# Gated mix of two linear attentions: output weights of two tiles at once on row halves, rows of r by block, small products of G as filler

## The chip, the core and the metric

The kernel runs on one core of one Trainium2 chip. The metric is the device time of one execution in microseconds; the figure before is the median of three runs.

## What is computed

Two linear-attention branches A and B read the same x (2048 rows, 640 features, bfloat16), each with weights of its own; a gate of each row mixes their outputs.

```python
H = 32; Dh = D // H                      # D = 640, so 20 features a head
q, k, v = split(x @ wqkv)                # each [S, H, Dh]
phi = lambda t: where(t > 0, t + 1, exp(t)) + 1e-6
pq, pk = phi(q), phi(k)
kv = einsum("bhsd,bhse->bhde", pk, v)
z = einsum("bhsd->bhd", pk)
num = einsum("bhqd,bhde->bhqe", pq, kv)
den = einsum("bhqd,bhd->bhq", pq, z)[..., None] + 1e-6
branch = (num / den).reshape(B, S, D) @ wo
...
g = sigmoid((x * gate_w).sum(-1, keepdims=True))
return g * branch_A + (1 - g) * branch_B
```

## The kernel before, in words

The value projection is never computed for all rows. Since v = x Wv, the kernel forms G = xT pk (640 x 640, tile GT) from x and the feature map of the keys (PK), then M = GT Wv (m_part), masks M to the heads (tile MG, by a constant in CB), and multiplies by the output weights wo. The result, WP, is a 640 x 640 matrix a branch, and the output is the feature map of the queries (PQ), scaled by gate / denominator, times WP. That factor of a row and a head is called r.

Stages, in the order in which TensorE runs them:

- Keys (k_part, k_tile): for each of 16 row tiles of 128 rows and each branch, x times Wk; ScalarE takes the exponential (EK), VectorE finishes PK.
- Queries (q_tile, L505): for each branch, four blocks of 512 rows and five feature tiles k, one tile of PQ. Feature tiles 0 to 3 take every second column of Wq (tile_of, L399), so that the tiles of a pair share one layout of heads over the partitions. WQ is loaded in one transfer a branch.
- G of A (g_piece, L543) is mixed in between the query tiles. A row-block j of G has four pieces q; one piece is four row tiles, each a 512- and a 128-column matmul. After the last piece ScalarE copies the block into GT.
- Sum z of the keys: GpSimd adds the 16 tiles of PK (z_add, L565), and z_turn (L575) spreads the sum over partitions with five small matmuls.
- The chains of L922 place what follows around the pieces of G of B: after its first piece z_turn of B and M of A (m_part, L718); after its second wp_a_den (L905): output weights of A (wp_tile, L747) with the denominators of both branches (den, L639) between them, then reciprocals, tables and widening, which use no TensorE. The remaining 18 pieces of G of B follow.
- wp_tile forms one of five feature tiles of WP: for each of two column halves of 320, four matmuls of 80 rows and 32 output columns on four column strips of the array, each for one window w of heads. ScalarE copies the first half out of PSUM, VectorE the second.
- r: VectorE takes the reciprocals (recip), SP writes them to a table in DRAM with five copies of each row (table), and reads them back repeated over the partitions (widen, L687): three issues for the first block of 512 rows, three for the other three blocks together, for each branch. scale (L699) multiplies PQ by it, block by block, in two VectorE instructions.
- Output (fin_mm, L792): row tiles 0 to 3 do A and B apart: A's part is copied to TA by ScalarE (fin_a) and added when B's is copied out (fin_out); later tiles sum ten products in one group. fin_pp picks the PSUM pair. A, t = 0 and 1, come first, then M of B, A t = 2, the output weights of B, A t = 3, then B t = 0 to 3 and tiles 4 to 15.

The order on each engine is the order in the program, and the scheduler (_Sched) puts in the waits from the keys that each operation reads and writes. All reads of PSUM by ScalarE and VectorE count as writes of the bank. L292 is the matmul of every stage (helper mms), L281 the DMA issue of every load (helper dma), so groups on the page go by tiles. PSUM has eight banks; pair i is banks 2i and 2i + 1.

Of the kernel before, what the change touches and what calls it, by code (L numbers as in the profile page):

```python
# [11 lines left out]
S = 2048  # L12
# [17 lines left out]
W = 80  # L30
HS = (0, 3, 6, 9, 12, 16, 19, 22, 25, 28)
PAD = DH * HS[-1] + 128 - D

# [12 lines left out]
def _build_consts():  # L46
    cd = np.zeros((128, C_W), dtype=np.float32)
    p = np.arange(128)[:, None]
    f = np.arange(64)[None, :]
    for w in range(NW):  # L50
        assert HS[w] <= 64 * w // DH and (64 * w + 63) // DH < HS[w] + W // DH <= H
        cd[0:W, C_MK + 64 * w : C_MK + 64 * w + 64] = (HS[w] + p // DH == (64 * w + f) // DH)[0:W]
    for k in range(NC):
        head = (512 + p if k == 4 else 256 * (k // 2) + 2 * p) // DH
        cd[:, C_ZM + 32 * k : C_ZM + 32 * k + 32] = head == np.arange(32)[None, :]
    return _bf16_bits(cd)
# [136 lines left out]
def bass_gated_mix__linear_attn_block__linear_attn_block__prompt_kernel(  # L193
# [20 lines left out]
    with ExitStack() as es:  # L214
        E = es.enter_context

        def sb(name, shape, dtype=dt.bfloat16):
# [11 lines left out]

        WVF = {X: sb("WV" + X, [128, NC * D + PAD]) for X in BR}  # L230
        WV = {X: WVF[X][:, 0 : NC * D].rearrange("p (c f) -> p c f", c=NC) for X in BR}
# [6 lines left out]
            "A": PK["A"][:, 0:10, :].rearrange("p t f -> p (t f)")[:, 0 : 3 * S].rearrange("p (i n) -> p i n", i=3),  # L238
            "B": XT[:, 0:3, :],
        }  # L240
        RX_LAP = {
            "A": [("PK", "A", t) for t in range(10)],
            "B": [("XT", t, c) for t in range(NT) for c in range(3)],
# [3 lines left out]
        MG = sb("MG", [W, NW, 64])  # L247
# [77 lines left out]
        def wo_at(X, w):  # L325

            if X == "A":
                Y = BR[w // NC]
                return WK[Y][0:W, w % NC, 0:D], ("WK", Y, w % NC)
            if w < NC:  # L330
                return WQ["A"][0:W, w, :], ("WQ", "A")
            return PK["A"][0:W, 6 + w, :], ("PK", "A", 6 + w)

        def load_wo(eng, X, w):
            o, key = wo_at(X, w)
            r0 = DH * HS[w]
            dma(eng, "wo%s%d" % (X, w), o, wo[X][r0 : r0 + W, :], writes=[("WO", X, w), key])
# [24 lines left out]
        for X in BR:  # L362
            pool(lambda e, X=X: e.memset(WVF[X][:, NC * D : NC * D + PAD], 0.0), writes=[("WVP", X)])
# [27 lines left out]
        load_w("SP", "wqA", WQ["A"], wqkv["A"][:, 0:D], ("WQ", "A"))  # L391
# [4 lines left out]
        load_w("SP", "wqB", WQ["B"], wqkv["B"][:, 0:D], ("WQ", "B"))  # L396
        load_w("SP", "wvB", WV["B"], wqkv["B"][:, 2 * D : 3 * D], ("WV", "B"))

        def tile_of(row, k):  # L399

            return row[:, 512:D] if k == 4 else row[:, 256 * (k // 2) + k % 2 : 256 * (k // 2) + 256 : 2]
# [103 lines left out]
        def q_tile(X, b, k):  # L505
# [7 lines left out]
                reads=xt_reads(4 * b, 4 * b + 4) + [("WQ", X)],  # L513
# [29 lines left out]
        def g_piece(X, j, q, pp):  # L543
            P = PP[pp]
            bks = [("PS", 2 * pp), ("PS", 2 * pp + 1)]
            steps = []
            for t in range(4 * q, 4 * q + 4):
                l = XN[:, t, 128 * j : 128 * j + 128]
                steps.append((P[:, 0:512], l, PK[X][:, t, 0:512], t == 0, t == NT - 1, None))
                steps.append((P[:, 512:D], l, PK[X][:, t, 512:D], t == 0, t == NT - 1, None))  # L550
            mms(
                steps,
                reads=[("XN", t) for t in range(4 * q, 4 * q + 4)] + [("PK", X, t) for t in range(4 * q, 4 * q + 4)],
                writes=bks,
                name="g%s%d%d" % (X, j, q),
            )
            if q == 3:
                act(
                    lambda e: e.activation(GT[:, j, :], P[:, 0:D], ACT.Copy),
                    reads=bks,  # L560
                    writes=[("GT", j)],
                )


        def z_add(X, t, pace=()):  # L565
            xi = BR.index(X)
            a = PK[X][:, 0, :] if t == 1 else ZS[:, :]
            o = ZP[:, xi, :] if t == NT - 1 else ZS[:, :]
            pool(
                lambda e: e.tensor_tensor(out=o, in0=a, in1=PK[X][:, t, :], op=ALU.add),  # L570
# [416 lines left out]
```

## Time and profile before

| | us |
|---|---|
| runs (three) | 191.35, 191.59, 192.03 |
| median | 191.59 |
| the profiled execution | 190.99 |
| its span | 189.7 |

The page counts time from the span's start. Idle time of an engine that is not on the chain of waits costs nothing. The busy rows of the other engines around the change, by form (busy us, mean ns, then idle time and its releaser):

```profile
L518 ACT ACTIVATE EQ<-ps 128x512 bf16<-128x512 f32 x40 | 23.9, 597 | 34.1 <-PE ps L292 34.0
L831 DVE CAST OSTG<-ps 128x640 bf16<-128x640 f32 x11 | 9.1, 826 | 14.8 <-PE ps L292 14.8
L559 ACT ACTIVATE GT<-ps 128x640 bf16<-128x640 f32 x10 | 7.0, 704 | 19.8 <-PE ps L292 19.8
L704 DVE TENSOR_TENSOR PQA<-PQA,PKA 128x2048 bf16<-128x2048 bf16 x4 | 4.9, 1217 | 5.9 <-DMA PKA<-rsA 5.9
L669 DVE RECIPROCAL RCA<-DTA 128x128 bf16<-128x128 f32 x4 | 3.4, 906 | 0.0
L767 DVE CAST WPB<-ps 128x320 bf16<-128x320 f32 x5 | 2.1, 482 | 1.2 <-PE ps L292 1.2
L767 ACT ACTIVATE WPB<-ps 128x320 bf16<-128x320 f32 x5 | 1.8, 447 | 2.3 <-PE ps L292 2.3
L737 DVE TENSOR_TENSOR MG<-ps,CB 80x512 bf16<-80x512 f32 x2 | 1.4, 687 | 6.4 <-PE ps L292 6.4
L737 DVE TENSOR_TENSOR MG<-ps,CB 80x128 bf16<-80x128 f32 x2 | 0.6, 277 | 0.0
```

And the transfers: KB each, median us from issue to landing.

```profile
PKA<-rsA SPq DMA_DIRECT2D x3, 384.0 KB, 4.0
XT<-rsB SPq DMA_DIRECT2D x3, 384.0 KB, 6.0
WKB<-in_B_wqkv_dram SPq DMA_DIRECT2D x1, 800.0 KB, 6.7
WQA<-in_A_wqkv_dram SPq DMA_DIRECT2D x1, 800.0 KB, 6.1
...
rsA<-RCA SPq DMA_DIRECT2D x4, 160.0 KB, 2.7
...
PKA<-rsA SPq DMA_DIRECT2D x3, 128.0 KB, 2.8
XT<-rsB SPq DMA_DIRECT2D x3, 128.0 KB, 3.4
...
gd<-SG SPq DMA_DIRECT2D x2, 8.0 KB, 15.6
...
WKB<-in_gate_w_dram SPq DMA_DIRECT2D x1, 1.2 KB, 6.7
```

### The profile page before, as it was taken

Reading aid. Unit: us, or ns where it says so; the run is one execution under the profiler, and the core shown is the slowest. Engines: PE = TensorE matmul, PEld = TensorE weight load, DVE = VectorE, ACT = ScalarE, POOL = GpSimd, SP = SyncE. Lnnn points to the kernel's source line nnn. Section 1 sums busy time; section 2 is a strip of 40 time slices with the busy share of each in tenths; the row PEclk is TensorE's granted clock in tenths of the full one; section 3 lists DMA queues with packets and bytes.
Section 4 is the critical chain, followed back from the end, with each engine's and each line's share of the span. In section 5 each row is a group of like instructions: output and inputs, shape, how many; then the busy total and the mean of one; then the engine's idle time right before and its main releaser. Section 6 shows DMA issues by size and latency. Waiting matters only on the chain.

```text
span 189.7 us, 3514 instructions
## 1 busy us (share of the span) xinstructions
PE 185.4 (98%) x1408; PEld 103.3 (54%) x1433; DVE 123.0 (65%) x212; ACT 65.8 (35%) x119; POOL 44.7 (24%) x38
## 2 busy tenths in 40 slices
PE   8999999999999999999999999999999999999995
PEld 5655555555444454545444457555557555555554
DVE  0398999998986674847767663891331885566223
ACT  3465565555643533533444422212213600000000
POOL 1000223253225656556637430000000000000000
DMA  5983449996335002111000003019596012111112
GB/s 188 321 115 84 110 94 324 365 362 202 100 13 1 0 14 56 63 46 43 3 0 2 0 3 108 5 40 220 163 288 236 3 73 103 69 46 58 73 69 69
DMA packets 27177, 19.61 MB, mean 103 GB/s; under 512 B 14296, under 2 KB 26136, under 8 KB 27160
## 3 DMA queue, kind: packets, MB, share of 16 engines
q1 hardware_dynamic: 26440, 18.66, 36.1%
q10 hardware_dynamic: 720, 0.72, 1.1%
q8 instruction: 11, 0.18, 0.4%
q14 instruction: 6, 0.05, 0.1%
HBM read 13.46 MB, written 3.95 MB: 92 GB/s over the span
## 4 chain that ended last, share of the span: by engine, by line
PE 94%; DVE 3%; ACT 1%; issue 1%
PE ps L292 93%; DVE PKA L493 2%; DVE EK L488 1%; PE ps L424 1%; ACT WPB L767 1%; DVE PKB L493 0%; ACT EK L477 0%; DVE OSTG L831 0%
## 5 line engine op out<-in xcount | busy, mean ns | idle before, releaser
L518 ACT ACTIVATE EQ<-ps 128x512 bf16<-128x512 f32 x40 | 23.9, 597 | 34.1 <-PE ps L292 34.0
L477 ACT ACTIVATE EK<-ps 128x640 bf16<-128x640 f32 x32 | 22.3, 704 | 16.1 <-PE ps L292 15.2
L523 DVE TENSOR_SCALAR EQ<-EQ 128x512 bf16<-128x512 bf16 x40 | 15.2, 380 | 18.0 <-ACT EQ L518 17.2
L292 PE MATMUL ps<-WPB,PQB 128*128 128x512 bf16 (+4 forms) x165 | 26.0, 295 | 0.0
L292 PE MATMUL ps<-WPA,PQA 128*128 128x128 bf16 (+4 forms) x158 | 25.0, 291 | 0.5 <-ACT WPB L767 0.2
L570 POOL TENSOR_TENSOR ZS<-ZS,PKA 128x640 f32<-128x640 f32 x13 | 18.8, 1446 | 27.2 <-DVE PKB L493 12.1
L292 PE MATMUL ps<-PKA,XN 128*128 128x128 bf16 (+1 forms) x156 | 24.5, 297 | 0.2
L292 PE MATMUL ps<-XT,WQB 128*128 128x512 bf16 x99 | 23.2, 379 | 0.1
L292 PE MATMUL ps<-WKA,XT 128*128 128x128 bf16 (+1 forms) x157 | 22.6, 298 | 0.2
L292 PE MATMUL ps<-XT,WQA 128*128 128x512 bf16 x97 | 22.6, 379 | 0.2
L570 POOL TENSOR_TENSOR ZS<-ZS,PKB 128x640 f32<-128x640 f32 x13 | 19.1, 1470 | 13.5 <-DVE PQB L528 11.0
L292 PE MATMUL ps<-WKB,XT 128*128 128x512 bf16 (+1 forms) x157 | 22.1, 297 | 0.2
L292 PE MATMUL ps<-PKB,XN 128*128 128x512 bf16 (+1 forms) x156 | 21.7, 297 | 0.3 <-issue 0.2
L831 DVE CAST OSTG<-ps 128x640 bf16<-128x640 f32 (+2 forms) x13 | 9.8, 754 | 16.1 <-PE ps L292 16.1
L292 PEld LDWEIGHTS ps<-PKA,XN 128*128 128x128 bf16 x160 | 13.1, 98 | 11.7
L292 PEld LDWEIGHTS ps<-WPA,PQA 128*128 128x128 bf16 x165 | 13.3, 98 | 9.3
L292 PEld LDWEIGHTS ps<-WPB,PQB 128*128 128x128 bf16 x165 | 13.3, 98 | 9.0
L292 PEld LDWEIGHTS ps<-WKB,XT 128*128 128x128 bf16 x160 | 12.4, 97 | 9.6
L292 PEld LDWEIGHTS ps<-PKB,XN 128*128 128x128 bf16 x160 | 12.2, 98 | 9.5 <-issue 0.3
L292 PEld LDWEIGHTS ps<-WKA,XT 128*128 128x128 bf16 x160 | 12.3, 98 | 9.2
L488 DVE TENSOR_SCALAR EK<-EK 128x640 bf16<-128x640 bf16 x32 | 14.6, 457 | 2.6 <-ACT EK L477 2.4
L292 PEld LDWEIGHTS ps<-XT,WQA 128*128 128x128 bf16 x100 | 9.4, 98 | 10.6
(64 smaller groups left out, 150.4 us busy)
## 6 DMA issues: line engine op xcount, KB each, us to landing
out_dram<-OSTG SPq DMA_DIRECT2D x15, 160.0 KB, 1.8
XN<-in_A_x_dram SPq DMA_DIRECT2D x3, 640.0 KB, 8.2
PKA<-rsA SPq DMA_DIRECT2D x3, 384.0 KB, 4.0
XT<-rsB SPq DMA_DIRECT2D x3, 384.0 KB, 6.0
WKB<-in_B_wqkv_dram SPq DMA_DIRECT2D x1, 800.0 KB, 6.7
WQA<-in_A_wqkv_dram SPq DMA_DIRECT2D x1, 800.0 KB, 6.1
WVA<-in_A_wqkv_dram SPq DMA_DIRECT2D x1, 800.0 KB, 9.6
WQB<-in_B_wqkv_dram SPq DMA_DIRECT2D x1, 800.0 KB, 11.3
```

Source lines behind the costliest of these rows:

```text
L292: ins = pe.matmul(o, l, r, start=st, stop=sp, tile_position=tp)
L424: ins = pe.transpose(dst[:, 128 * i : 128 * i + 128], XN[:, t, 128 * c : 128 * c + 128], IDN[:, :],)
L477: lambda e: e.activation(EK[:, slot, :], P[:, 0:D], ACT.Exp),
L488: lambda e: e.tensor_scalar(EK[:, slot, :], EK[:, slot, :], 1.0, EPS, op0=ALU.min, op1=ALU.add),
L493: lambda e: e.scalar_tensor_tensor(out=PK[X][:, t, :], in0=P[:, 0:D], scalar=0.0, in1=EK[:, slot, :], op0=ALU.max, op1=ALU.add),
L518: lambda e: e.activation(EQ[:, slot, :], bank(bk, 0, 512), ACT.Exp),
L523: lambda e: e.tensor_scalar(EQ[:, slot, :], EQ[:, slot, :], 1.0, EPS, op0=ALU.min, op1=ALU.add),
L570: lambda e: e.tensor_tensor(out=o, in0=a, in1=PK[X][:, t, :], op=ALU.add),
L767: lambda e, o=o, p=p, j=j: e.tensor_copy(o, p) if j else e.activation(o, p, ACT.Copy),
L831: dve(lambda e, o=o, p=p: e.tensor_copy(o, p), reads=bks, writes=keys)
```

## The change

- Feature order: tiles 0 to 3 of the queries are now whole runs of 128 columns of a permuted WQ. The permutation (blocks of 64 columns) is made by the load: load_wq issues seven transfers a branch in place of one. z_add's last sum (to ZP) is written in the same order: five GpSimd instructions of 128 columns instead of one of 640.
- Windows of M: ten windows of 128 rows instead of 80, each holding 32 columns of two feature tiles that stand on the upper and the lower 64 rows (_pair, _start). M's matmuls are as many as before; MG has 128 partitions.
- Output weights: wp_tile gives way to wp_mm and wp_out. Tiles 0 and 1, and 2 and 3, are formed at once, one on rows 0 to 63 and one on rows 64 to 127, four strips each, into different banks; tile 4 alone, at full height. Column pieces are 512 and 128 instead of 320 and 320. The copies of A are all on ScalarE; those of B are shared between ScalarE and VectorE.
- Order around A: z_turn of B; the 16 small (128-column) matmuls of G of B, block 0; M of A; denominators of A; output weights of A; denominators of B; the 16 large matmuls of that block; the other four blocks of G.
- Rows of r: widen issues nine parts for each branch and each of the blocks 0, 1, and 2 with 3. For blocks 0 and 1 four of the nine are issued on ScalarE, each four after a copy of G; the others on SP. The widened r covers all five feature tiles, and scale is one instruction. Blocks A 0, B 0 and A 1 are scaled ahead of the output of A, B 1 behind the output weights of B.
- Output: fin_mm puts each matmul in as an operation of its own, which waits for its own slice of PQ and WP. fin_pp and fin_a change banks and halves for A, t = 2 and 3.
- The wo weights of B are loaded into both WQ tiles, chunk by chunk, instead of WQ of A and part of PK of A.

```diff
-W = 80
-HS = (0, 3, 6, 9, 12, 16, 19, 22, 25, 28)
-PAD = DH * HS[-1] + 128 - D
+FRONT = 4
+PAD = 48
+def _feature(k, p):
+    return 512 + p if k == 4 else 256 * (k // 2) + 128 * (p // 64) + 64 * (k % 2) + p % 64
+def _heads(x):
+    return 32 * x // DH, (32 * x + 31) // DH
+def _pair(m):
+    return 4 * (m // 2) + m % 2
+def _start(m):
+    a = _pair(m)
+    (a0, a1), (b0, b1) = _heads(a), _heads(a + 2)
+    lo = max(DH * a1 + DH - 64, DH * b1 + DH - 128)
+    hi = min(DH * a0, DH * b0 - 64)
+    assert lo <= hi
+    return min(max(lo, D - 128), hi) if lo > D - 128 else hi
 ...
+        def load_wq(X):
+            for o, i, n in ((0, 0, 1), (1, 2, 1), (2, 1, 1), (3, 3, 2), (5, 6, 1), (6, 5, 1), (7, 7, 3)):
+                dma(
+                    "SP",
+                    "wq%s%d" % (X, o),
+                    WQ[X][:, :, 64 * o : 64 * o + 64 * n],
+                    wqkv[X][:, 64 * i : 64 * i + 64 * n].rearrange("(c p) f -> p c f", p=128),
+                    writes=[("WQ", X, b) for b in range(o, o + n)],
+                )
+        def wo_at(X, m):
 
             if X == "A":
-                Y = BR[w // NC]
-                return WK[Y][0:W, w % NC, 0:D], ("WK", Y, w % NC)
-            if w < NC:
-                return WQ["A"][0:W, w, :], ("WQ", "A")
-            return PK["A"][0:W, 6 + w, :], ("PK", "A", 6 + w)
-        def load_wo(eng, X, w):
-            o, key = wo_at(X, w)
-            r0 = DH * HS[w]
-            dma(eng, "wo%s%d" % (X, w), o, wo[X][r0 : r0 + W, :], writes=[("WO", X, w), key])
+                Y = BR[m // NC]
+                return WK[Y][:, m % NC, 0:D], ("WK", Y, m % NC)
+            Y = BR[m // NC]
+            return WQ[Y][:, m % NC, :], ("WQC", Y, m % NC)
+        def load_wo(eng, X, m):
+            o, key = wo_at(X, m)
+            r0 = _start(m)
+            p0, p1 = max(0, -r0), min(128, D - r0)
+            dma(eng, "wo%s%d" % (X, m), o[p0:p1, :], wo[X][r0 + p0 : r0 + p1, :], writes=[("WO", X, m), key])
+            if p0:
+                dma(eng, "wf%s%d" % (X, m), o[0:p0, :], wo[X][0:p0, :], writes=[("WOF", X, m)])
 ...
         def tile_of(row, k):
-            return row[:, 512:D] if k == 4 else row[:, 256 * (k // 2) + k % 2 : 256 * (k // 2) + 256 : 2]
+            return row[:, 128 * k : 128 * k + 128]
 ...
+        def g_run(X, j, pp, units, out=False):
             P = PP[pp]
-            bks = [("PS", 2 * pp), ("PS", 2 * pp + 1)]
             steps = []
-            for t in range(4 * q, 4 * q + 4):
-                l = XN[:, t, 128 * j : 128 * j + 128]
-                steps.append((P[:, 0:512], l, PK[X][:, t, 0:512], t == 0, t == NT - 1, None))
-                steps.append((P[:, 512:D], l, PK[X][:, t, 512:D], t == 0, t == NT - 1, None))
+            for t, h in units:
+                cs = slice(512, D) if h else slice(0, 512)
+                steps.append((P[:, cs], XN[:, t, 128 * j : 128 * j + 128], PK[X][:, t, cs], t == 0, t == NT - 1, None))
+            ts = sorted({t for t, h in units})
 ...
+        RX_PARTS = [(k, e, 64 * (k // 2) + 16 * (k % 2) + 32 * e, 16) for k in range(4) for e in (0, 1)] + [(4, 0, 128, 32)]
+        def widen(eng, X, b0, b1, parts):
             c0, c1 = 512 * b0, 512 * b1
-            for i, (g0, n) in enumerate(maps):
+            for k, e, g0, n in parts:
                 dma(
-                    "SP",
-                    "rx%s%d%d" % (X, b0, i),
-                    RXW[X][:, i, c0:c1],
-                    rs[X][g0 : g0 + n, c0:c1].unsqueeze(1).to_broadcast([n, 128 // n, c1 - c0]),
+                    eng,
+                    "rx%s%d%d%d" % (X, b0, k, e),
+                    RXW[X][64 * e : 64 * e + 4 * n, k, c0:c1],
+                    rs[X][g0 : g0 + n, c0:c1].unsqueeze(1).to_broadcast([n, 4, c1 - c0]),
                     reads=[("RS", X, b) for b in range(b0, b1)],
-                    writes=[("RX", X, i, b) for b in range(b0, b1)],
+                    writes=[("RX", X, k, e, b) for b in range(b0, b1)],
                 )
 
         def scale(X, b):
             cols = slice(512 * b, 512 * b + 512)
-            pairs = RXW[X][:, 0:2, cols]
-            v = PQ[X][:, 0:4, cols].rearrange("p (i a) n -> p i a n", i=2)
+            v = PQ[X][:, :, cols]
+            dve(
+                lambda e: e.tensor_tensor(out=v, in0=v, in1=RXW[X][:, :, cols], op=ALU.mult),
+                reads=[("RX", X, k, e, b) for k, e, _, _ in RX_PARTS] + RX_LAP[X],
+                writes=[("PQ", X, b, k) for k in range(NC)],
+            )
 ...
+        def m_part(X, m0, m1, bk):
+            n = m1 - m0
+            steps = []
+            for m in range(m0, m1):
+                d0 = FRONT + _start(m)
+                steps += acc(
+                    bank(bk, 64 * (m - m0), 64 * (m - m0) + 64).rearrange("p (h f) -> p h f", h=2),
+                    [
+                        (
+                            WVF[X][:, D * j + d0 : D * j + d0 + 128],
+                            GT[:, j, 128 * (m // 2) : 128 * (m // 2) + 128].rearrange("p (h q f) -> p h q f", h=2, q=2)[
+                                :, :, m % 2, :
+                            ],
+                        )
+                        for j in range(NC)
 ...
+        def wp_mm(X, lo, hi, places):
+            steps, ms = [], set()
+            for k, (bk, c) in places.items():
+                for g in range(4):
+                    if k == 4:
+                        m, r0, r1, h = 8 + g % 2, 0, min(128, D - _start(8 + g % 2)), g // 2
+                    else:
+                        m, r0, r1, h = 4 * (k // 2) + g, 64 * (k % 2), 64 * (k % 2) + 64, k % 2
+                    ms.add(m)
+                    steps.append(
+                        (
+                            bank(bk, c, c + hi - lo, 32 * g, 32 * g + 32),
+                            MG[r0:r1, m, 32 * h : 32 * h + 32],
+                            wo_at(X, m)[0][r0:r1, lo:hi],
+                            True,
+                            True,
+                            (r0, 32 * g),
+                        )
 ...
+        def wp_out(eng, X, ks, lo, hi, bk, c=0):
+            n = len(ks)
+            p = bank(bk, c, c + n * (hi - lo))
+            o = WP[X][:, ks[0], lo:hi]
+            if n > 1:
+                p = p.rearrange("p (k f) -> p k f", k=n)
+                o = WP[X][:, ks[0] : ks[-1] + 1 : ks[1] - ks[0], lo:hi]
+            (dve if eng == "DVE" else act)(
+                lambda e: e.tensor_copy(o, p) if eng == "DVE" else e.activation(o, p, ACT.Copy),
+                reads=[("PS", bk)],
+                writes=[("WP", X, k, lo // 512) for k in ks],
+            )
 ...
-            return {"A": (2, 1), "B": (0, 3)}[X][t % 2]
+            return {"A": (2, 1, 2, 2), "B": (0, 3, 0, 3)}[X][t]
 ...
+                ks = [(Y, k) for Y in X for k in range(NC)]
+                for i, (Y, k) in enumerate(ks):
+                    mms(
+                        [
+                            (
+                                bank(bk, 0, hi - lo),
+                                PQ[Y][:, k, 128 * t : 128 * t + 128],
+                                WP[Y][:, k, lo:hi],
+                                i == 0,
+                                i == len(ks) - 1,
+                                None,
+                            )
+                        ],
+                        reads=[("PQ", Y, t // 4, k)] + [("WP", Y, k, j) for j in (0, 1) if (hi > 512 if j else lo < 512)],
+                        writes=[("PS", bk)],
+                        name="fin%s%d" % (X, t),
+                    )
 ...
-        nA = len(mains)
-        for j in range(NC):
+        late = []
+        for j in range(1, NC):
             for q in range(4):
-                mains.append(lambda j=j, q=q: g_piece("B", j, q, j % 2))
-        def wp_a_den():
-            wp_tile("A", 0, 1)
-            wp_tile("A", 1, 2)
-            den("A", 6)
-            wp_tile("A", 2, 1)
-            den("B", 7)
-            wp_tile("A", 3, 2)
-            wp_tile("A", 4, 1)
-            for X in BR:
-                for i in range(4):
-                    recip(X, i)
-                for b in range(NB):
-                    table(X, b)
-            for b0, b1 in ((0, 1), (1, NB)):
-                for X in BR:
-                    widen(X, b0, b1)
-        chains = [
-            _Chain(nA - 20, [(0, lambda: z_turn("A", 7))]),
-            _Chain(nA, [(0, lambda: [load_wo("SP", "B", w) for w in range(NW)])]),
-            _Chain(nA, [(0, lambda: z_turn("B", 7))]),
-            _Chain(nA, [(0, lambda: [m_part("A", 0, 8, 2), m_part("A", 8, NW, 3)])]),
-            _Chain(nA + 1, [(0, wp_a_den), (15, lambda: scale("A", 0))]),
-        ]
-        _interleave(mains, chains)
+                late.append(lambda j=j, q=q: g_piece("B", j, q, j % 2))
+        _interleave(mains, [_Chain(len(mains) - 20, [(0, lambda: z_turn("A", 7))])])
+        for m in range(NW):
+            load_wo("SP", "B", m)
+        z_turn("B", 7)
+        g_run("B", 0, 0, [(t, 1) for t in range(NT)])
+        m_part("A", 0, 8, 2)
+        m_part("A", 8, NW, 3)
+        den("A", 7)
+        wp_mm("A", 0, 512, {4: (4, 0)})
+        wp_mm("A", 512, D, {4: (1, 384)})
+        wp_mm("A", 0, 512, {0: (2, 0), 1: (3, 0)})
+        wp_mm("A", 0, 512, {2: (5, 0), 3: (6, 0)})
+        wp_mm("A", 512, D, {0: (1, 128), 1: (0, 0)})
+        wp_mm("A", 512, D, {2: (1, 256), 3: (0, 128)})
+        wp_out("ACT", "A", (4,), 0, 512, 4)
+        wp_out("ACT", "A", (0,), 0, 512, 2)
+        wp_out("ACT", "A", (1, 3), 512, D, 0)
+        wp_out("ACT", "A", (0, 2, 4), 512, D, 1, 128)
+        for k, bk in ((1, 3), (2, 5), (3, 6)):
+            wp_out("ACT", "A", (k,), 0, 512, bk)
+        for X in BR:
+            if X == "B":
+                widen("SP", "A", 0, 1, RX_PARTS[0:2])
+                den("B", 4)
+            for i in range(4):
+                recip(X, i)
+            for b in range(NB):
+                table(X, b)
+        g_run("B", 0, 0, [(t, 0) for t in range(NT)], True)
+        widen("ACT", "A", 0, 1, RX_PARTS[2:6])
+        widen("SP", "A", 0, 1, RX_PARTS[6:])
+        groups = [("B", 0), ("A", 1), ("B", 1)]
+        for X, b in groups:
+            widen("SP", X, b, b + 1, RX_PARTS[4:])
+        for X in BR:
+            widen("SP", X, 2, NB, RX_PARTS)
+        for i, fn in enumerate(late):
+            fn()
+            if i % 4 == 3 and groups:
+                X, b = groups.pop(0)
+                widen("ACT", X, b, b + 1, RX_PARTS[:4])
+        for X, b in (("A", 0), ("B", 0), ("A", 1)):
+            scale(X, b)
         for t in (0, 1):
             fin_mm(t, "A")
             fin_a(t)
-        scale("B", 0)
         m_part("B", 0, 8, 7)
         m_part("B", 8, NW, 6)
         fin_mm(2, "A")
-        for k in range(NC):
-            wp_tile("B", k, (0, 3, 1)[k % 3])
-        fin_a(2)
-        scale("A", 1)
+        fin_a(2, True)
+        wp_mm("B", 0, 512, {4: (7, 0)})
+        wp_mm("B", 512, D, {4: (6, 256)})
+        wp_mm("B", 0, 512, {0: (0, 0), 1: (1, 0)})
+        wp_mm("B", 0, 512, {2: (2, 0), 3: (3, 0)})
+        wp_mm("B", 512, D, {0: (6, 0), 1: (5, 0)})
+        wp_mm("B", 512, D, {2: (6, 128), 3: (5, 128)})
+        wp_out("DVE", "B", (4,), 0, 512, 7)
+        wp_out("ACT", "B", (1,), 0, 512, 1)
+        wp_out("DVE", "B", (0,), 0, 512, 0)
+        wp_out("ACT", "B", (1, 3), 512, D, 5)
+        wp_out("DVE", "B", (2,), 0, 512, 2)
+        wp_out("ACT", "B", (3,), 0, 512, 3)
+        wp_out("DVE", "B", (0, 2, 4), 512, D, 6)
+        scale("B", 1)
         fin_mm(3, "A")
         fin_a(3)
-        later = {1: ("B", 1), 3: ("A", 2), 5: ("B", 2), 7: ("A", 3), 9: ("B", 3)}
+        later = {3: ("A", 2), 5: ("B", 2), 7: ("A", 3), 9: ("B", 3)}
         for t in range(NT):
             fin_mm(t, "B" if t < APART else "AB")
             fin_out(t)
```

## The prediction

> **What bounds it now.** I read the page's engine shares first, then the chain of waits in order of time, then the timeline of the two places that the diff touches, then the forms of the groups there and the DMA rows.
>
> ```profile
> span 189.7 us, 3514 instructions
> PE 185.4 (98%) x1408; PEld 103.3 (54%) x1433; DVE 123.0 (65%) x212; ACT 65.8 (35%) x119; POOL 44.7 (24%) x38
> ```
>
> TensorE (PE) is busy for 98% of the span; every other engine has a third or more free. So only what shortens PE's own stream, or its few gaps, can help, and only what makes PE wait can hurt. The chain from 116 us on:
>
> ```profile
> 116.67 4.68 PE ps L292 x87
> 121.35 0.16 issue
> 121.51 6.74 PE ps L292 x49
> ...
> 145.25 1.58 PE ps L292 x13
> 146.83 0.02 issue
> 146.85 1.43 ACT WPB L767 x4
> 148.29 0.12 issue
> 148.41 6.74 PE ps L292 x49
> ```
>
> Columns: start, length, what. The chain leaves PE once after the start-up: 1.43 us in which ScalarE copies the output weights of B, with PE waiting between. From 121.51 to the next piece of the chain at 128.30 are 6.79 us for 25 pairs of a 512- and a 128-column matmul (49 are recorded; one record in fifty is missing all through): 0.272 us a pair, so 0.217 for 512 columns, 0.136 for 320, 0.054 for 128. The timeline of the stage of B:
>
> ```profile
> 146.11 0.44 PE L292 MATMUL ps<-WPA,PQA 128*128 128x128 bf16 x5
> 146.48 0.85 PE L292 MATMUL ps<-WQA,MG 80*32 80x320 bf16 x17
> ...
> 147.54 0.72 PE L292 MATMUL ps<-PKA,MG 80*32 80x320 bf16 x11
> 148.18 1.36 PEld L292 LDWEIGHTS ps<-WPA,PQA 128*128 128x128 bf16 x10
> 148.41 1.31 PE L292 MATMUL ps<-WPA,PQA 128*128 128x512 bf16 x9 [0.16 <-ACT WPB L767]
> ```
>
> Forty matmuls of 320 columns run as ten groups of four column strips side by side. Between 146.48 and the last group's start (148.26 less the 0.31 of one matmul: 147.95) lie nine steps: 1.47 us, where nine times 0.136 would be 1.22. Of the excess I take 0.22 for the wait on the copies, since the starts in the timeline (147.04, 147.17, 147.34, 147.53) stay 0.13 apart until 147.17 and widen after it. Entering strips costs 0.09 (the last full matmul starts at 146.33, the first strip 0.15 later instead of 0.05). Leaving costs 0.12: ten weight loads stand beside nine recorded matmuls, so the first matmul after it belongs to the load at 148.18 and starts near 148.20, 0.25 after the last group instead of 0.136.
>
> **The change, part by part, on PE.** (1) *Output weights on row halves.* Per branch 10 x 0.136 = 1.36 us becomes three groups of 512 and three of 128 columns, where two tiles use the upper and lower 64 rows at once: 3 x 0.217 + 3 x 0.054 = 0.81, saving 0.54. No row shows row halves running together. The bounds are 0.81 (fully) and five tiles x 0.272 = 1.36 (not at all). I take 0.86: the nearest rows, the strips, overlap fully (20 matmuls of 512 columns in 1.25 us at 118.19), and the 0.05 is for eight weight loads behind a group of only 0.054. (2) *Mode changes.* A runs denominators at full height, row halves, denominators again: two more changes than before; B has one more. At the 0.09 to 0.12 of the two rows: 0.2 and 0.1. Bounds: 0, and the tail of a 512-column matmul, 0.379 - 0.217 = 0.16 each.
>
> The Trainium skill (TensorEngine Tiling, Key Properties) says that changing the tiling mode drains TensorE. The two rows above agree with a partial drain of 0.09 and 0.12 us; no run here shows a change between full height and row halves. Were each of the three a full 0.16, the sum below would be 0.18 us smaller.
>
> (3) *Waits in B.* The copies now start with whole 512-column halves on both engines, the next tile of A uses banks 4 and 5 that were emptied before, and each output matmul waits only for its own slice. PE needs slice 0 of B near 148.6; VectorE's rows (0.482 for 320 columns, 0.826 for 640, so 0.69 for 512) have it at 147.9, slice 2 at 148.6 (needed 149.0), the last 128-column slices at 149.2 (needed 149.6). So the 0.22 goes, with 0.4 us to spare each. If that margin went, the loss would be one-for-one. (4) *A's new wait.* The denominators of B write bank 4 and so wait for ScalarE's copy of tile 4: 0.38 (matmul) + 0.05 + 0.60 (the 128x512 row of L518) + 0.05 = 1.08 after the stage starts, where PE arrives after 0.86 + 0.2 = 1.06. Cost 0.02 to 0.3; I take 0.05. The large half of G's first row-block needs bank 0, free after ScalarE's third copy at about 2.1; PE arrives at 2.3. (5) *Filler.* G of B, block 0, is the same 32 matmuls; its 16 small ones (16 x 0.054 = 0.9 us) stand ahead of M of A, which needs the copy of G of A that ended at 114.69; PE is there at 114.8. The denominators (1.08) cover the copies of MG (0.69 + 0.28) as a G piece did. Nothing gained or lost. (6) *fin B, t = 2* reuses the pair of t = 0. That is emptied near 151.1, behind the scaling of B block 1 (1.5) on VectorE; PE comes at 151.3. Margin 0.15, bound 0.3; I take 0.05.
>
> Sum: A -0.54 + 0.05 + 0.2 + 0.05 = -0.24; B -0.54 + 0.05 + 0.1 - 0.22 + 0.05 = -0.56; together **-0.8**.
>
> **What is moved off PE.** Rows of r go from 12 to 54 issues, 16 of them on ScalarE. Four earlier issues on SP:
>
> ```profile
> 131.53 1.89 SPq L281 DMA_DIRECT2D PKA<-rsA  x3
> 133.47 3.18 SPq L281 DMA_DIRECT2D XT<-rsB  x3
> 136.78 1.81 SPq L281 DMA_DIRECT2D PKA<-rsA  x3
> 138.70 1.83 SPq L281 DMA_DIRECT2D XT<-rsB  x3
> ```
>
> Mostly 0.62 us an issue, once 1.06 in a triple. Denominators of A come at 117.5, four reciprocals (0.9 each) end near 121.9, the tables of A are issued there, those of B from 125.9 to 128.5 after B's reciprocals. On SP then follow 3 pieces for A block 0, 5 for B 0, 5 for A 1 (13 x 0.62: 136.5), 5 for B 1, 18 for the rest (to 150.8, before the first output issue at 151). With 3 us to land (the rows say 2.8 and 3.4), A 1 is there at 139.5. VectorE runs scale A 0, B 0, A 1 in order and behind them the copies of MG of B. PE, at fin A near 140.5, wants scale A 0 then (done near 135) and MG by 146.0, so scale A 1 must start by 143.6: 4.1 us of slack hide it. On ScalarE four issues (2.5 us) fit between copies of G, which come every 4.35 us and take 0.70. Cost taken: 0.
>
> Query weights in seven loads per branch of 128- to 384-byte runs instead of one: SP stays 3.7 us longer at 27 us. Small runs are cheap: the gate column (640 runs of 2 bytes) was issued 0.5 us behind WKB and lands after the same 6.7 us, so about 0.5 us for 640 runs. WQ of A would be complete by 38, needed from 49. Upper bound, the store of gd (2048 elements in 15.6 us, 7.6 ns each): the last blocks at 61, 8 us late. I take 0. POOL's last add in five parts: ZP of B was ready at 110.8, needed at 113.8; even 2 us for the parts is hidden. Scaling in one instruction saves 0.1 us on VectorE, off the path.
>
> **Against the runs.** The profiled execution took 190.99 us, 1.3 outside its span; the sum gives 190.2 for it. The median of the runs shown is 191.59, 0.6 above, so I forecast 191.59 - 0.8 = **190.8**. A measurement of this kernel can tell about 0.3% (0.57 us) from no change.
>
> **Rivals.** *Row halves don't overlap* (0.12): stages stay at 1.36, three more mode changes add 0.3, the 0.22 still goes: 191.7. For: no row shows it; against: strips overlap perfectly. *Copies out of PSUM decide* (0.10): PE waits 0.3 for bank 4 and 0.3 for the pair of t = 0, instead of the 0.1 counted: 191.3. For: margins of 0.02 and 0.15; against: both engines share the copies.
>
> The Trainium skill (TensorEngine Tiling, PSUM Bottleneck) warns that tiling speeds TensorE but not the emptying of PSUM. The trace agrees in B, where PE waits 0.22 us on the copies.
>
> *Rows of r come late* (0.19), the slower side: at 1.06 us an issue, the thirteen on SP end at 142.3, A 1 lands 3.4 later at 145.7, scale and MG copies take 2.4: 148.1, where PE stands at 146.0. PE loses 2.1: 192.9. It decides once an issue costs above 0.93 us (4.1 / 13 more than 0.62). For: issues rise from 12 to 54, one triple ran at 1.06; against: each moves half as many rows. *Query weights late* (0.05): by the gd rate, up to 8 us of stall around 53 us; 195 or more.
>
> **How the numbers follow.** Forecast 0.54 with its own range 190.1 to 191.3: 0.45 of it beyond 0.3%, 0.09 within. Copies: 0.03 faster, 0.07 same. No overlap: 0.10 same, 0.02 slower. Late rows and late weights: 0.24 slower. Faster 0.48, same 0.26, slower 0.26. The low end, 190.0, has free mode changes and full overlap and 0.3 of scatter; the high end, 192.9, takes in the late rows.
>
> **What would show it.** Right: groups of eight 32-wide matmuls starting within 0.03 us, 0.22 apart for 512 columns; PE at fin A near 140.5 instead of 140.85 and at fin B near 148.6 instead of 149.6; no 1.43 on ScalarE in the chain. Wrong: groups of four in halves one after the other; the copies of MG of B starting after 145; SP issues above 0.9 us; PE idle near 49 to 55 us.

## The result, and the profile after

Six runs of the changed kernel have a median of **190.69 us** (190.63 to 191.05), six of the kernel before, beside them, 191.88 (191.35 to 192.14): ratio 0.9951 [0.9932, 0.9970]. Two repeats gave 0.9945 [0.9924, 0.9966] and 0.9951 [0.9934, 0.9967]. So the change makes the kernel faster, by some 0.9 to 1.0 us of 191.6.

The profiled execution took 190.64 us, against 190.99 before: only 0.35 less. What the two profiles lack of the 0.9 is not in the stages, as is shown below. The page's span and engine shares:

```profile
span 189.4 us, 3591 instructions
PE 185.1 (98%) x1409; PEld 102.8 (54%) x1433; DVE 121.0 (64%) x199; ACT 66.7 (35%) x119; POOL 45.9 (24%) x48
```

TensorE is as full as before, so the gain is in the work that its stream no longer holds. The chain of waits (start, length, what), the pieces from the third tile of A's output on, through the stage of B:

```profile
145.58 2.36 PE ps L318 x49
147.94 0.16 issue
148.10 6.74 PE ps L318 x49
```

The 1.43 us of ScalarE's copies of WPB are gone from it; there is nothing but TensorE here, with 0.16 us ("issue") in which it waited for nothing that the profile shows. The stage of A in TensorE's timeline (start, length, then line, operation, operands, form and count):

```profile
118.05 0.45 PE L318 MATMUL ps<-WKB,MG 128*32 128x512 bf16 x8
118.43 0.60 PE L318 MATMUL ps<-WKA,MG 64*32 64x512 bf16 x9
118.66 0.38 PE L318 MATMUL ps<-WKB,MG 64*32 64x512 bf16 x3
118.67 0.38 PE L318 MATMUL ps<-WKA,MG 64*32 64x512 bf16 x1
118.67 0.38 PE L318 MATMUL ps<-WKB,MG 64*32 64x512 bf16 x3
118.87 0.27 PE L318 MATMUL ps<-WKA,MG 64*32 64x128 bf16 x9
...
119.14 1.26 PE L318 MATMUL ps<-PQB,ZBD 128*32 128x512 bf16 x20
```

The rows with `64*32` are the row halves. Eight of the nine matmuls at 118.43 are the first group; the ninth and the seven of the three rows behind it are the second. By the single starts, the eight of a group start within 0.025 us, and the groups of 512 columns are 0.216 to 0.227 apart. Two tiles do run for the time of one. The stage of B, and the first output matmuls of B behind it:

```profile
146.82 0.46 PE L318 MATMUL ps<-WQB,MG 128*32 128x512 bf16 x8
147.20 0.60 PE L318 MATMUL ps<-WQA,MG 64*32 64x512 bf16 x9
...
148.10 1.31 PE L318 MATMUL ps<-WPA,PQA 128*128 128x512 bf16 x9 [0.16 <-issue]
149.24 1.95 PE L318 MATMUL ps<-WPB,PQB 128*128 128x512 bf16 x12
```

To compare executions I cut each at four starts of TensorE: the first matmul after G of A (113.79 before, 114.36 after), the first output matmul of A (140.85, 141.19), the first of B (149.56, 149.24), and the last matmul (187.57, 187.26). Between them, in us, with repeats of both kernels:

| stretch | before | again | after | again | third | change | predicted |
|---|---|---|---|---|---|---|---|
| A | 27.069 | 27.068 | 26.826 | 26.825 | 26.824 | -0.243 | -0.24 |
| B | 8.700 | 8.700 | 8.052 | 8.050 | 8.052 | -0.648 | -0.56 |
| outputs | 38.015 | 38.016 | 38.016 | 38.016 | 38.016 | 0 | 0 |

The stretches repeat within 0.002 us, and their sum, -0.89, is the change. The rest of an execution varies: the first stretch begins at 113.79 and 114.33 in two profiles of before, at 114.36, 114.07 and 114.87 in three of after. The first profile of before was an early one and the first of after a late one, and that took 0.58 us off the difference. The change does not need the later start: run 2 below, an edit of the changed kernel, begins its first stretch at 113.79 too. All of the 0.58 is there when ScalarE begins its first exponential, at 8.42 us before and 8.99 after. One matmul of TensorE's timeline ahead of that, of before, then of after:

```profile
3.99 0.22 PE L292 MATMUL ps<-const-bfloat16-1.0 128*128 128x128 bf16 x1
```

```profile
4.09 0.31 PE L318 MATMUL ps<-const-bfloat16-1.0 128*128 128x128 bf16 x1
```

The same matmul of 128 columns takes 0.22 us in the one and 0.31 in the other. By the spacing of such matmuls, 0.107 us and then 0.056, TensorE came to its full rate near 3.9 us in the one execution and after 5.3 us in the other.

### The profile page after: what moved, and what is told of

Read it like the earlier page. It is cut to its first block, busy times and chain, and to the rows that moved or that the text cites. A ratio compares the mean times of both kernels' runs of the same rounds, so it can differ in the third digit from the quotient of the medians.

```text
span 189.4 us, 3591 instructions
## 1 busy us (share of the span) xinstructions
PE 185.1 (98%) x1409; PEld 102.8 (54%) x1433; DVE 121.0 (64%) x199; ACT 66.7 (35%) x119; POOL 45.9 (24%) x48
## 4 chain that ended last, share of the span: by engine, by line
PE 94%; DVE 3%; issue 1%; ACT 0%
PE ps L318 93%; DVE PKA L533 2%; PE ps L464 1%; DVE EK L528 1%; DVE PKB L533 0%; ACT EK L517 0%; DVE OSTG L929 0%
## 5 line engine op out<-in xcount | busy, mean ns | idle before, releaser
L318 PE MATMUL ps<-PKB,XN 128*128 128x128 bf16 (+1 forms) x157 | 21.7, 297 | 0.3 <-issue 0.2
```

The lines of the kernel that those rows point to most:

```text
L318: ins = pe.matmul(o, l, r, start=st, stop=sp, tile_position=tp)
```

## The experiments

All but the first, ninth and tenth are edits of the changed kernel. An interval in brackets is that of the ratio to the kernel before, timed beside it.

**1. The kernel before, unchanged.** Is the 0.35 us between the two profiles the change, or chance at the start?

> The kernel before once more, unchanged. Theory (the length of the start is chance): from the first steady matmul of the keys to the last matmul 172.6 us as in its first profile, and the start before that anywhere between the two starts seen (full matmul rate from 3.9 us in the profile of before, from 5.6 us in that of after, 0.58 us apart at the end of the start). Rival (the change itself lengthened or shortened the start): the start is that of the first profile of before again, to 0.1 us. The time: within 0.3% of the kernel before.

Measured: 191.59 us, ratio 1.0000 [0.9982, 1.0017]; stretches of 27.068, 8.700 and 38.016; the first begins at 114.33, not 113.79. An unchanged kernel moves by 0.55 us at its start and by 0.001 in its stages, so the stages are what can be compared.

**2. Output weights at full height**, still in the new order, with the new banks and each output matmul waiting for its own slice. Two tiles of a pair now follow each other instead of running at once.

```diff
-                        m, r0, r1, h = 4 * (k // 2) + g, 64 * (k % 2), 64 * (k % 2) + 64, k % 2
+                        m, r0, r1, h = 4 * (k // 2) + g, 0, 128, k % 2
```

> The changed kernel with tiles 0 to 3 of the output weights formed at full height, one after the other (the masked half of MG is zero, so the sum is the same). Theory (row halves pay 0.54 us a branch less their mode changes): the stage from the first small matmul of G of B to the output of A grows from 26.83 to 27.1 us (0.54 more, 0.26 of mode changes less), the stage from there to the output of B from 8.05 to 8.5; together 0.7 us longer than the changed kernel, ratio to before about 0.999. Rival (the gain is the order and the removed waits alone): both stages as in the changed kernel to 0.1 us.

Measured: 191.60 us, 1.0002 [0.9987, 1.0018]; A 27.083, B 8.473. The row halves, net of their mode changes, are worth 0.257 in A and 0.421 in B. What is left of the change in B, 8.700 to 8.473 = 0.227, is the wait on the copies: in this run the ten groups of B start 0.216 and 0.056 apart, without the wider steps of the kernel before. In A nothing is left but +0.014. By the medians all of the gain goes; by the stages 0.21 of it stays, which the interval cannot tell from none.

**3. Output matmuls that wait for all slices.** The new order and the row halves stay; every output matmul waits for all copies of the weights and all scaled rows of its block, as it would with one wait for the whole.

```diff
-                        reads=[("PQ", Y, t // 4, k)] + [("WP", Y, k, j) for j in (0, 1) if (hi > 512 if j else lo < 512)],
+                        reads=[("PQ", Z, t // 4, c) for Z in X for c in range(NC)] + [("WP", Z, c, j) for Z in X for c in range(NC) for j in (0, 1)],
```

> The changed kernel, each output matmul waiting for all slices as before the change. Theory (each slice's own wait hides the last copies): the first output matmul of B waits for the last copy, which ended 0.38 us after that matmul's start in the changed kernel; 0.4 to 0.5 us longer than the changed kernel, all of it in the stage from the output of A to the output of B (8.5 instead of 8.05). Rival (A's fourth tile covers the copies anyway): 8.05, no change.

Measured: 190.77 us, 0.9966 [0.9950, 0.9983]; B 8.487, which is 0.435 more than with a wait for each slice; A is the same. TensorE's timeline of this run, where the outputs of B begin:

```profile
149.39 1.96 PE L318 MATMUL ps<-WPB,PQB 128*128 128x512 bf16 x12 [0.27 <-DVE WPB L845]
```

The bracket is the idle time ahead of the row and what ended it: the last copy on VectorE, which the changed kernel leaves standing beside TensorE's first output matmuls (it ends there at 149.62, and they begin at 149.24). The bracket counts from the end of the matmul before, 0.16 us behind the time at which the next could have started: 0.27 and 0.16 are the 0.43. Shorter matmuls alone would have run into the copies; the waits for single slices are what lets them be short.

**4. No filler.** The 16 small products of G of B, block 0, no longer stand ahead of M of A; all 32 follow the denominators of B.

```diff
-        g_run("B", 0, 0, [(t, 1) for t in range(NT)])
...
-        g_run("B", 0, 0, [(t, 0) for t in range(NT)], True)
+        g_run("B", 0, 0, [(t, h) for t in range(NT) for h in (0, 1)], True)
```

> The changed kernel without the small matmuls of G of B ahead of M of A: all 32 of that block stand behind the denominators. Theory (they cover the copy of G of A): M of A waits for that copy, 0.8 us of TensorE idle between z and M, stage of A 27.6 instead of 26.83 us, the run 0.8 us longer. Rival (M could start at once): 26.8, no change.

Measured: 191.27 us, 0.9998 [0.9979, 1.0016]; A 27.717, +0.891, which is the 0.9 us of the sixteen. TensorE's timeline of this run:

```profile
114.06 0.28 PE L318 MATMUL ps<-ONE,ZP 128*128 128x32 bf16 x5
115.11 1.62 PE L318 MATMUL ps<-GT,WVA 128*128 128x64 bf16 x50 [0.77 <-ACT GT L599]
```

Without them TensorE stands 0.77 us before M of A, until ScalarE has copied G of A. M of A starts 1.048 us into the stretch here and 1.049 in the changed kernel: in both it starts 0.14 us behind the end of that copy. The copy in the changed kernel, where M starts at 115.41:

```profile
114.56 0.70 ACT L599 ACTIVATE GT<-ps 128x640 bf16<-128x640 f32 x1 [1.52 <-PE ps L318]
```

So the sixteen fill the wait almost, but not wholly: between the last of them and M lie 0.086 us instead of a step of 0.056, and 0.03 us of waiting is left. The kernel before put a whole piece of G of B there and started M at 1.215 without a wait. The filler is cover that was kept and no gain of its own; without it the gain of the whole change is lost.

**5. Denominators of both branches together.** The denominators of B go right behind those of A (both are strips), so that the change from halves back to strips falls away; the 128-column pieces go first, so that bank 0 is emptied early. `den` is split for it: `den_b()` puts VectorE's part for B where it was.

```diff
         den("A", 7)
+        den_b = den("B", 6, True)
...
-        wp_mm("A", 0, 512, {0: (2, 0), 1: (3, 0)})
-        wp_mm("A", 0, 512, {2: (5, 0), 3: (6, 0)})
         wp_mm("A", 512, D, {0: (1, 128), 1: (0, 0)})
         wp_mm("A", 512, D, {2: (1, 256), 3: (0, 128)})
+        wp_mm("A", 0, 512, {0: (2, 0), 1: (3, 0)})
+        wp_mm("A", 0, 512, {2: (5, 0), 3: (7, 0)})
+        wp_out("ACT", "A", (1, 3), 512, D, 0)
...
-                den("B", 4)
+                den_b()
```

> The changed kernel with the denominators of B directly behind those of A, and the 128-column pieces of the output weights of A ahead of the 512-column ones. Theory (the return from row halves to full-height strips costs 0.16 us, and the wait on bank 4 is in it): stage of A 26.67 instead of 26.83 us, the rest as in the changed kernel, 0.1 to 0.2 us shorter than the changed kernel. Rival (TensorE then waits for ScalarE's copy out of bank 0 instead): 26.8 or longer.

Measured: 190.63 us, 0.9953 [0.9935, 0.9971]; A 26.847. The rival was right: the saved mode change is eaten by a wait. The weight loads of this run:

```profile
120.03 0.98 PEld L318 LDWEIGHTS ps<-PKB,XN 128*128 128x128 bf16 x6 [0.61 <-ACT WPA L850]
```

G's next row-block needs bank 0, and ScalarE's copy out of it is now the last thing that TensorE waits for. In the changed kernel the 1.08 us of B's denominators stand between and hide it.

**6. The same, with bank 0 copied by two engines**: the piece of 128 columns of tile 3 on VectorE, that of tile 1 on ScalarE.

```diff
-        wp_out("ACT", "A", (1, 3), 512, D, 0)
+        wp_out("ACT", "A", (1,), 512, D, 0)
+        wp_out("DVE", "A", (3,), 512, D, 0, 128)
```

> As dens_together, but bank 0 is emptied by two engines at once: ScalarE copies 128 columns, VectorE the other 128 ahead of its reciprocals. Theory (in dens_together TensorE stood about 0.2 us for the 0.39 us copy out of bank 0, which ate the mode change saved): bank 0 free near 5.8 us after the stage's start instead of 6.0, stage of A 26.65 to 26.70 instead of 26.83 us; the rows of r come 1 us later, which the 1.4 us of slack ahead of MG of B hold; 0.15 us shorter than the changed kernel in the trace. Rival (the saved mode change is not there at all): 26.83 or longer. Second rival (the later rows cost): the stage of B above 8.05.

Measured: 191.03 us, 0.9975 [0.9956, 0.9993]; A 27.065, worse by 0.24. Its VectorE timeline:

```profile
119.97 0.29 DVE L850 CAST WPA<-ps 128x128 bf16<-128x128 f32 x1 [1.19 <-ACT WPA L850]
```

The premise failed: the program orders two readers of one bank behind each other. VectorE was idle for 1.19 us and began only behind ScalarE's copy (119.66 to 119.93); the bank came free at 120.26, which is, counted from the start of the stretch, 0.22 later than in run 5. Whether two copies at once would have saved the mode change was not tried.

**7. All issues of the rows of r on SP**, in the order of blocks; ScalarE issues none of its 16. Does the four-issue share on ScalarE carry its weight?

```diff
-        widen("ACT", "A", 0, 1, RX_PARTS[2:6])
-        widen("SP", "A", 0, 1, RX_PARTS[6:])
+        widen("SP", "A", 0, 1, RX_PARTS[2:])
...
-            widen("SP", X, b, b + 1, RX_PARTS[4:])
+            widen("SP", X, b, b + 1, RX_PARTS)
...
-                widen("ACT", X, b, b + 1, RX_PARTS[:4])
+                pass
```

> The changed kernel with all 54 issues of rows of r on SP, block by block. By the issue rate of the changed kernel (0.65 us) A block 1 then lands about 6.5 us later, at 149.5 us. Theory (the slack is what the profile after shows: VectorE idle 0.8 us ahead of the copies of MG and 0.6 until TensorE needs them, 1.4 us): TensorE loses 5 us ahead of the output weights of B. Rival (the slack is the 4.1 us of the prediction): it loses 2.4 us. Third (rows are off the path): no loss.

One execution: 198.31 us; B 14.153 (+6.1), outputs 39.844 (+1.8). Two rows of VectorE's timeline, then two of TensorE's:

```profile
148.64 1.49 DVE L769 TENSOR_TENSOR PQA<-PQA,PKA 128x2560 bf16<-128x2560 bf16 x1 [3.97 <-DMA PKA<-rsA]
169.15 0.82 DVE L924 TENSOR_TENSOR OSTG<-ps,PKB 128x640 bf16<-128x640 f32 x1 [8.83 <-DMA out_dram<-OSTG]
```

```profile
151.07 0.46 PE L318 MATMUL ps<-WQB,MG 128*32 128x512 bf16 x8 [4.43 <-DVE MG L799]
170.03 1.25 PE L318 MATMUL ps<-WPA,PQA 128*128 128x512 bf16 x5 [1.16 <-DVE OSTG L924]
```

The chain in B is the one of the prediction's rival of late rows: late rows, late scaling of A block 1, the copies of MG queued behind it on VectorE, TensorE idle. It cost 4.50 us against the changed kernel, near the 5 that were expected; the other 1.60 of B's 6.10 came behind the wait, where TensorE's matmuls of 512 columns were 0.427 us apart until 155.1 (as in the next run, with the granted clock beside it). The 1.83 in the outputs is a second chain, at full rate: SP is busy with rows until 165.8, so the first outputs are issued only then, VectorE waits 8.83 us for a free staging buffer, and TensorE 1.33 between two starts at 170.03; the late scaling of a block of B's queries behind it costs another 0.46, at 174.30.

**8. All sixteen ScalarE issues at once**, right behind the first copy of G of B, instead of four after every fourth.

```diff
         widen("ACT", "A", 0, 1, RX_PARTS[2:6])
+        for X, b in (("B", 0), ("A", 1), ("B", 1)):
+            widen("ACT", X, b, b + 1, RX_PARTS[:4])
...
             if i % 4 == 3 and groups:
-                X, b = groups.pop(0)
-                widen("ACT", X, b, b + 1, RX_PARTS[:4])
+                groups.pop(0)
```

> The changed kernel with all 16 of ScalarE's issues directly behind its first copy of G of B. Theory (an issue occupies ScalarE 0.63 us, and the queue waits for the tables of B): the second copy of G comes near 138 us instead of 128.3, TensorE, which needs that pair again at 133, waits 5 to 6 us. Rival (an issue costs ScalarE nothing that TensorE feels): no loss.

One execution: 199.19 us; A 35.056 (+8.2), B and outputs the same. The timelines of ScalarE (the 13.49 us ahead of the copy hold the sixteen issues and their wait for the tables of B) and of TensorE, and the windows, which give the stretch, its length, the busy time of the five engines and, last, granted clock, DMA share and GB/s:

```profile
138.57 1.30 ACT L599 ACTIVATE GT<-ps 128x640 bf16<-128x640 f32 x2 [13.49 <-issue]
```

```profile
139.33 7.85 PE L318 MATMUL ps<-PKB,XN 128*128 128x512 bf16 x44 [6.35 <-ACT GT L599]
```

```profile
140.00:142.00 2.00, 2.00 (x10) 0.90 (x8) 1.48 (x1) 0.00 (x0) 0.00 (x0) 0.50 0.75 214
142.00:144.00 2.00, 2.00 (x14) 1.02 (x13) 1.21 (x2) 0.00 (x0) 0.00 (x0) 0.79 0.19 56
```

The second copy of G came at 138.57, as expected (near 138). But an idle of 6.35 us cost 8.2: behind it the granted clock is 0.50, matmuls of 512 columns start 0.427 apart instead of 0.216, and full rate is back only near 142.9, which is 1.7 of the 8.2. Both expectations, of 7 and of 8, lacked this term.

**9 and 10. The changed kernel again, twice**, beside runs 5 and 6:

> The changed kernel once more, beside the next one on the same chip. From the first steady matmul of the keys to the last matmul 171.7 us as in its first profile; the time 0.9 to 1.2 us below the kernel before, the part over 0.9 being the start, if the start is chance.

> The changed kernel beside it. Stages 26.83, 8.05 and 38.02 us again; the run 0.1 to 0.2 us above dens_two_copies by the theory, equal by its rival.

Measured: 190.59 and 190.86 us, against 191.54 and 191.67; their ratios and stages are in the first section. No variant was faster than the changed kernel.

## Why the prediction was right

Forecast -0.8; by the stages -0.89, by the three comparisons -0.94, -1.05 and -0.94 us (ratios times 191.6). The mechanism was as stated, and the two stretches each came near their own sum. Two things are luck. That the median, 190.69, lies 0.11 from the forecast of 190.8 owes something to the runs: the kernel before, beside it, was at 191.88 and not at 191.59. And that A came within 0.003 of its sum is two misses that cancel: the row halves did 0.04 better than taken, the mode changes with the wait on bank 4 were 0.01 worse, and 0.03 of waiting ahead of M was not in the sum. Step by step:

- **Row halves** overlap in full. Taken: 0.86 us a branch, with 0.05 of it for eight weight loads behind a short group. Measured: groups 0.216 to 0.227 apart at 512 columns and 0.056 at 128; the loads cost at most 0.011 in all. This 0.05 was oversized in both branches.
- **Mode changes.** Taken: 0.1 each. Measured from the starts: strips to halves 0.160 where a step of 128 columns is 0.056, so 0.104, in A and in B. From halves back to the denominators' strips in A: 0.216, so 0.16, with the wait on bank 4 in it: the first of these weight loads starts 0.05 behind the end of ScalarE's copy of tile 4, as the weight load of run 5 does behind the copy that it waits for. So the wait decided, and this change's own cost is hidden in it. Two changes and that wait were taken at 0.25 and measure 0.264. The Trainium skill (TensorEngine Tiling (Array Packing), Key Properties) says that a change of the tiling mode drains TensorE; the trace agrees that it costs, with 0.104 here, below the 0.16 tail of a whole matmul.
- **Waits in B.** Taken: -0.22. Measured by run 2: -0.227. Run 3 shows that it hangs on the wait for single slices, which is worth 0.435 now that the matmuls are shorter.
- **fin B, t = 2.** Taken: 0.05. The outputs' stretch is unchanged at 38.016, so it cost nothing. With the weight loads this is the 0.09 by which B did better than forecast.
- **Filler.** Taken: nothing lost or gained. Nearly right: run 4 puts 0.89 on it as a cover, and M waits 0.03 all the same. The prediction compared TensorE's arrival (114.8) with the end of the copy (114.69) and left out the 0.14 from the copy's end to M's first matmul.
- **Query weights, POOL's parts.** TensorE has no stall at the start of the queries and ZP's parts took 0.42 to 0.56 us each. The rival of late weights, and the one in which halves don't overlap, are both out. So is the one in which the copies decide: it had 0.3 us of waiting at bank 4, where 0.16 was lost with the mode change in it, and 0.3 at the pair of t = 0, where none was.
- **Rows of r.** Taken: no cost, with 4.1 us of slack. No cost was right; the slack was 1.4. Here are SP's queue and VectorE's timeline after:

```profile
127.67 2.51 SPq L307 DMA_DIRECT2D rsB<-RCB  x4
130.22 2.17 SPq L307 DMA_DIRECT2D PKA<-rsA  x3
...
135.88 4.74 SPq L307 DMA_DIRECT2D PKA<-rsA  x5
...
156.06 1.60 SPq L935 DMA_DIRECT2D out_dram<-OSTG  x3
```

```profile
143.01 1.49 DVE L769 TENSOR_TENSOR PQA<-PQA,PKA 128x2560 bf16<-128x2560 bf16 x1 [1.02 <-DMA PKA<-rsA]
145.28 0.89 DVE L799 TENSOR_TENSOR MG<-ps,CB 128x512 bf16<-128x512 f32 x2 [0.78 <-PE ps L318]
```

VectorE was idle for 0.78 us ahead of the copies of MG, and these ended at 146.17, 0.65 before TensorE used them at 146.82: 1.4 together. The step that was too small is "13 x 0.62: 136.5". The tables of B went out at 127.67 and not at 125.9: the reciprocals of B had ended at 126.43, SP was issuing until 126.67, and eight waits on semaphores for XT's buffers (127.12 to 127.60) stood ahead of the tables. The thirteen issues took 10.4 us, 0.80 each, with one of 1.70. The last ended at 140.6 and A 1 was there at 143.0, not 139.5. Of each of these delays 0.58 is the later start of the whole execution, which TensorE shares. Run 7 bears the 1.4 out: the scaling began 5.87 us later there, counted from the start of A's stretch, and TensorE lost 4.50, so 1.37 were slack. Run 7 is the rival of late rows carried out, run 8 another way to lose on the same issues, by late copies of G: TensorE waits 4.43 or 6.35 us. So the slower side was nearer than the 4.1 us suggested, and both the share on ScalarE and its spreading are needed.

**The signs.** The two starts named are met once the 0.58 is taken off: the output of A at 141.19 is then 140.61 (140.5 named), that of B at 149.24 is 148.66 (148.6). The sign of being wrong, copies of MG of B after 145, would be met as it stands (145.28), but is not with the start taken off (144.70); there VectorE waited for TensorE, not for rows. SP's issues took 0.80 us on average and not above 0.9.

Not in the forecast was one more wait: SP's rows end at 156.0 instead of 150.8, so the first outputs are issued at 156.06, and VectorE waited 4.95 us at 159.39 for a free staging buffer. The unchanged stretch of outputs shows that this cost nothing. Run 7 shows what the same wait costs when the rows end 10 us later still: 1.33 us.

## What to carry to other kernels

Where TensorE is 98% busy, read a change from the distance between fixed points of its stream: that repeats within 0.002 us, while the start-up alone moves the time by half a microsecond and more, so one profile against one profile can hide more than half of the gain. Shorter matmuls can run into what they had hidden: in B the waits for single slices were worth 0.44 us, as much as the row halves brought there (0.42), and in A the filler that keeps the copy of G covered was worth 0.89, against 0.26 for the row halves. Work that is moved to a queue at no cost still has a slack; compute it from the queue's measured average with its worst issue. A slack missed by several microseconds was paid for twice here, as idle time and as a slow clock after it.

## What was not expected of the hardware

**A long wait slows TensorE after it.** In run 8 TensorE stood for 6.35 us, to 139.33; the granted clock fell to 0.50 at 136.01, 3.0 us into the wait, and rose at 142.84, 3.5 us after work had begun again. In run 7 it stood for 4.43 us, to 151.07; the first two groups of 512 columns behind the wait still took 0.22 and 0.23 us, and only at 151.72 did the clock fall, to rise at 155.14. So the clock was at 0.50 for 6.83 and 3.41 us, which cost 1.7 and 1.6 us on top of the waits. The 0.77 us of run 4 had no such effect. The Trainium skill (TensorE: Matmul & The Clock Gate, Part 1: The HAM clock gate) says that TensorE falls to half its clock after an idle window of about 3.4 us and returns to full after as long a busy one, with windows that run on their own; these two runs agree in the lengths, one and two times 3.41 us, and in that the fall came at a time of its own. They do not show how much work such a window may hold: the 3.4 us ahead of the fall in run 7 held 0.65 us of matmuls. The spread at the start looks like the same rule, which no run here settles: there the profile's clock row shows 1.00 throughout while the spacing is doubled, so it is read from the spacing alone, and waits of 0.15 to 0.19 us on the first loads add to it in some executions.

**Eight small matmuls at once.** Eight tiles of 64 rows by 32 columns ran as one: groups of 512 columns were 0.216 to 0.227 us apart, as four strips are (0.216 to 0.226), and a group of 128 columns started 0.056 behind the one before. Their eight weight loads cost at most the 0.011 us above.
